# From the tenth attention step on: a stated order for TensorE

## The chip, the cores and the metric

The kernel runs on one core of one Trainium2 chip. The metric is the device time of one execution in microseconds (us), as the median of several runs; lower is better. A profiled execution gives, beside its time, a trace of every instruction on the engines: TensorE (PE), VectorE (DVE), ScalarE (ACT), GpSimd (POOL) and SyncE (SP, which issues the transfers).

## What is computed

Four batches of eight heads of attention with a window and 32 global positions, a normalised gated feed-forward layer and a second feed-forward layer with a rational function between its products:

```python
# attention, per batch and head: 512 local and 32 global positions, 64 wide
s_g   = scale * q_g @ k_all.T                      # global rows see all 544 keys
out_g = softmax(s_g) @ v_all
s_l   = scale * q_l @ [k_g, k_l].T                 # local rows: the 32 global keys and |i-j| <= 32
out_l = softmax(masked s_l) @ [v_g, v_l]
x = concat(out_g, out_l) as (B*544, 8*64)          # 2176 rows of 512
# first feed-forward layer
xn = x / sqrt(mean(x*x) + 1e-6) * rms_g
x  = (silu(xn @ w_gate) * (xn @ w_val)) @ w_out    # d_ff 1536
# second
h = x @ w_in                                       # d_ff 2048
x = (P(h) / (Q(h) + 1e-6)) @ w_out2                # cubic over quadratic
```

## The kernel before

**Stages.** The work is in three stages: attention, the first feed-forward layer (class `FFN1`) and the second one (`ffn2`). The loop over `t` in `tile_attn_ffn_kernel` (L889) runs attention in steps and puts the first 58 units of `FFN1` among them (`IN_ATTN`, L878); the other units of `FFN1` follow from L931 on, when the memory of attention has been given to the next weights; then comes `ffn2`.

**Attention in steps.** There are 32 score sets (`NS`), each for two heads and 256 local rows. A set s goes through four parts: `scores` (PE products into psS, then four masked minima on DVE at L401 and four exponentials on ACT at L406), `trans` (four PE transpositions into psT, copied to `pt` by ACT at L413), `pv` (16 small PE products with the values into psO, divided on DVE at L431 to L434 into `on`) and `out` (two transpositions into psX, copied into `x` by ACT at L444). Before a set can start, `make_q` (psQ, copied on ACT) and, for the first four sets of a batch, `make_k` (psK, copied on DVE) have to run; `make_g` (psKG) does the same for a batch's global part, and `g_scores`, `g_trans`, `g_pv` and `g_out` (psG, psGT, psOg, psGX) compute two groups of global rows per batch. A step t of `step` (L519) makes the operands of set t, then takes set t-1 to part 2, set t to part 1, set t-2 to part 3 and set t-3 to part 4; the last steps, t up to 35, only finish what is open (`TAIL`, L146).

**Shapes on PE.** psT, psX, psQ, psK, psGT and all products of `FFN1` use the whole array (128*128 in the rows). psS uses it as tiles of 64*32, psO and psOg of 128*32, psG of 128*64. An attention product in plain float32 has two MATMUL records in the trace, so a whole psS or psO group is 16 products and 32 records.

**FFN1 in units.** A unit is 12 products: half of an `up` (six into psg and six into psv, L650 to L654; two units make one k of one block of rows) or one `down` (12 into psA, L678 to L680). After the second half of an `up`, `act` (L661 to L669) takes psg and psv through ACT (tanh, L665) and DVE (L666, L667) and splits the result in two parts, `ah` on ACT and `al` on POOL. A block's normalisation (`norm_stages`) sums squares on ACT and POOL (L609 to L615), puts the sum over partitions on PE (psN, L618), takes a power on ACT (L620) and six steps on DVE (L623 to L625), scales the four parts of `x` on DVE (L628); `split` then makes `xt` in two parts on ACT (L640) and POOL (L641). The blocks follow in the order 1, 0, 3, 2, 5, 4, 7, 6, twelve units each (eight in the first).

**Banks.** Eight PSUM banks are shared in three kinds: four "big" (psS, psG, psg, psv), two "t" (psT, psQ, psK, psX, psGT, psGX, psKG) and two "o" (psO, psOg, psA, psN). Who writes a bank waits until the engine that reads its last content is done.

**What sets the order.** The program is recorded in the order of the code, and a scheduler with its own estimate of times then places the instructions on each engine; `tc.high_priority` shifts some of them forward. `between()` (L874) puts a unit in where the target number for this step has not been reached. So, on PE, instructions of attention and of feed-forward units can stand between each other singly.

Of the kernel before, what the change touches and what calls it, by code (L numbers as in the profile page):

```python
# [19 lines left out]
B, H, SL, SG, D = 4, 8, 512, 32, 64  # L20
# [118 lines left out]
class Attention:  # L139
# [3 lines left out]

    NP = B * H // 2
    NS = 2 * NP
    TAIL = 4  # L146
    VW = 65

    def __init__(self, tc, pool, x, stage, q_l, k_l, v_l, q_g, k_g, v_g, more):
# [367 lines left out]
    def step(self, t, between):  # L517
# [30 lines left out]
        for q0, first in ((0, 4), (1, 5)):  # L548
            n = i - first
            if t < NS:  # L550
# [7 lines left out]
                if n == 2:  # L558
# [3 lines left out]
                    between()  # L562
                    self.g_out(qd)


class FFN1:

# [236 lines left out]
def kernel(  # L804
# [20 lines left out]
    def load_consts():  # L825
        nc.sync.dma_start(out=gam, in_=rms_g.rearrange("(c p) -> p c", p=128))
        nc.sync.dma_start(out=av, in_=bass.AP(tensor=ca.tensor, offset=ca.offset, ap=[[0, 128], [1, 4]]))
        nc.sync.dma_start(out=bv, in_=bass.AP(tensor=cb.tensor, offset=cb.offset, ap=[[0, 128], [1, 2]]))
# [24 lines left out]
    ORD = [2 * b + 1 - i for b in range(B) for i in range(2)]  # L853
    done = [0]
    norms = []
    silu = [False]

    def norm_step():
        if norms and next(norms[0], StopIteration) is StopIteration:
            norms.pop(0)  # L860

    def unit():
        done[0] += 1
        next(units, None)
# [5 lines left out]
    att = Attention(tc, apool, x, y[0].rearrange("p c t -> p (c t)"), q_l, k_l, v_l, q_g, k_g, v_g, more)  # L870
    target = [0]

    def between():
        if done[0] < target[0]:  # L874
            unit()

    LAST = att.NS + att.TAIL - 1
    START, SECOND, IN_ATTN = 5, 9, 58  # L878
    nc.scalar.preload_act_table_set("exp_and_others")
    ps_scope = ExitStack()  # L880
    pp = ps_scope.enter_context(tc.tile_pool(name="ps1", bufs=1, space=PSUM))
# [4 lines left out]
    ffn = FFN1(tc, f1pool, x, y, gam, wts)  # L886
    units = ffn.units([(g, blk, lambda: silu[0]) for g in range(3) for blk in ORD])
    ffn.set_psum(pp, ("big", banks[0]), ("o", banks[2]))
    for t in range(LAST + 1):  # L889
        if t >= SECOND:  # L890
            target[0] = 6 + (IN_ATTN - 6) * (t + 1 - SECOND) / (LAST + 1 - SECOND)
        elif t >= START:
            target[0] = 6 * (t + 1 - START) / (SECOND - START)
        gate = [i.ins for i in (att.last_exp, att.last_ttr) if i]
        with tc.high_priority(offset=50) if t >= START else nullcontext():
            att.step(t, between)
        while done[0] < target[0] - 1:
            unit()
        if t == 2:
            load_consts()  # L900
        if t % 4 == 2 and t > 12:
            norms.append(ffn.norm(ORD[(t - 6) // 4]))
        elif t in (4, 8):
            norms.append(ffn.norm(ORD[t // 4 - 1]))
        with tc.high_priority(offset=200):
            for _ in range(3):
                norm_step()
        for _ in range(2 if t else 0):
            if loads:
                loads.pop(0)()  # L910
        with ExitStack() as late:
            for i in gate if t <= 8 else ():
                late.enter_context(tc.issue_after(i))
            for _ in range((0, 0, 0, 2, 5, 4, 4, 4)[t] if t < 8 else 2):
                wts.step(nc.gpsimd)
    while done[0] < IN_ATTN:
        unit()
    ps_scope.close()
    attn_scope.close()

# [88 lines left out]
```

## Time and profile before

| | us |
|---|---|
| median of 3 runs | 1047.36 |
| lowest and highest | 1046.0, 1047.61 |
| the profiled execution, its own time | 1044.23 |
| the span of its instructions | 1042.5 |
| PE busy | 985.7 (95%) |
| DVE, ACT, POOL busy | 784.3, 595.0, 272.7 |

The profiled execution took 1.7 us more than the span of its instructions, and 3.1 us less than the median. In the trace the tenth step (t = 9) begins at about 92 us, the last product of attention (psX of set 31) stands at 287.70, and the first product of the first unit of which both programs have the same things before and after it on PE (the third `up` of block 4, psg_4_2) at 303.15. The stretch from 83.18 (psK of set 8's keys, up to where both programs have the same order) to 303.15 is the one in which the change moves PE's work; it holds 1925 products.

### The profile page before, as it was taken

The numbers are of one execution on the slowest core, as the hardware profiler recorded it, in microseconds if no ns is written. First come the engines' busy times: TensorE is split into PE (matmuls) and PEld (weight loads), VectorE is DVE, ScalarE is ACT, GpSimd is POOL, SyncE is SP. The second block draws the span as 40 slices with busy tenths as digits, with TensorE's granted clock in tenths as the row PEclk, the third lists the DMA queues.
The fourth block names the chain that finished last, engine by engine and source line by source line (L and its number), as shares of the span: only waits on it lengthen the run. The fifth ranks groups of instructions, "written<-read, shape, count | busy, mean of one in ns | idle before, by whom it ended". The sixth has DMA issues, their size and how long they took to land.

```text
span 1042.5 us, 21627 instructions
## 1 busy us (share of the span) xinstructions
PE 985.7 (95%) x8352; PEld 883.7 (85%) x8352; DVE 784.3 (75%) x1842; ACT 595.0 (57%) x1347; POOL 272.7 (26%) x337
## 2 busy tenths in 40 slices
PE   6488999999989999999999999999999999999997
PEld 5266777677789999999999998898989889888895
DVE  5776456546479898855885535898998989989897
ACT  4665556455476764544644323666666667666674
POOL 6344131222200000000000003343443444434433
PEclk9679999999989999999999999999999999999999
DMA  9735545353081413523501116000000000000000
GB/s 243 226 85 130 118 120 119 84 130 81 7 304 45 157 43 131 200 95 107 177 1 42 41 31 225 29 1 20 11 2 31 1 1 31 1 31 1 1 31 21
DMA packets 103303, 82.25 MB, mean 79 GB/s; under 512 B 63136, under 2 KB 90784, under 8 KB 103200
## 3 DMA queue, kind: packets, MB, share of 16 engines
q1 hardware_dynamic: 101472, 74.58, 24.5%
q0 software_dynamic: 1728, 6.29, 1.8%
q8 instruction: 66, 1.08, 0.5%
q14 instruction: 37, 0.30, 0.1%
HBM read 62.64 MB, written 10.75 MB: 70 GB/s over the span
## 4 chain that ended last, share of the span: by engine, by line
PE 60%; DVE 20%; ACT 7%; DMA 5%; POOL 4%; issue 2%; SPq 2%; ACTq 0%; POOLq 0%; DVEq 0%
PE psg L650 4%; PE psA L678 4%; PE psg L654 4%; PE psv L654 4%; PE psv L650 4%; PE psA L680 4%; PE psv L651 4%; PE psA L679 4%; PE psg L651 4%; DVE q L772 3%; DVE q L760 3%; DVE r L773 3%; DVE p L774 3%; PE psH L750 2%; PE psH L751 2%
## 5 line engine op out<-in xcount | busy, mean ns | idle before, releaser
L750 PE MATMUL psH<-yt,w_h 128*128 128x384 f32 (+1 forms) x384 | 126.0, 329 | 1.2 <-ACT yt L732 0.7
L751 PE MATMUL psH<-yt,w_h 128*128 128x384 f32 (+1 forms) x384 | 125.4, 327 | 0.0
L752 PE MATMUL psH<-yt,w_h 128*128 128x384 f32 (+1 forms) x384 | 123.4, 328 | 0.8 <-DVE yt L733 0.8
L678 PE MATMUL psA<-ah,w_o 128*128 128x288 f32 (+1 forms) x384 | 112.2, 295 | 4.9 <-ACT ah L668 1.8
L650 PE MATMUL psg<-xt,w_g 128*128 128x288 f32 (+1 forms) x384 | 113.9, 300 | 0.9 <-ACT xt L640 0.9
L134 POOL TENSOR_SCALAR gh<-p 128x384 fp32r<-128x384 f32 (+1 forms) x96 | 59.4, 618 | 209.5 <-DVE p L774 180.3
L785 PE MATMUL psB<-w_p,gh 128*128 128x512 f32 x272 | 108.2, 398 | 5.4 <-POOL gh L134 5.1
L650 PE MATMUL psv<-xt,w_v 128*128 128x288 f32 (+1 forms) x384 | 111.2, 292 | 0.5 <-ACT a L663 0.5
L651 PE MATMUL psv<-xt,w_v 128*128 128x288 f32 (+1 forms) x384 | 111.1, 291 | 0.0
L651 PE MATMUL psg<-xt,w_g 128*128 128x288 f32 (+1 forms) x384 | 110.8, 291 | 0.0
L776 POOL TENSOR_TENSOR gl<-p,gh 128x384 fp32r<-128x384 f32 (+1 forms) x96 | 108.4, 1129 | 8.4 <-PE psB L787 0.4
L679 PE MATMUL psA<-ah,w_o 128*128 128x288 f32 (+1 forms) x384 | 110.2, 290 | 0.0
L680 PE MATMUL psA<-al,w_o 128*128 128x288 f32 (+1 forms) x384 | 109.8, 290 | 0.0
L786 PE MATMUL psB<-w_p,gh 128*128 128x512 f32 x272 | 107.2, 394 | 0.0
L654 PE MATMUL psv<-xt,w_v 128*128 128x288 f32 (+1 forms) x384 | 105.0, 293 | 0.0
L654 PE MATMUL psg<-xt,w_g 128*128 128x288 f32 (+1 forms) x384 | 104.7, 294 | 0.0
L770 ACT ACTIVATE r<-q,cq 128x384 f32<-128x384 f32 (+1 forms) x96 | 57.4, 598 | 63.5 <-DVE q L760 62.6
L91 POOL TENSOR_SCALAR raw_h<-raw_h 128x512 int32<-128x512 uint32 x1 | 0.6, 647 | 335.0 <-DMA raw_h<-in_moe_w_in_dram 335.0
L760 DVE SCALAR_TENSOR_TENSOR q<-q,bv,t 128x384 f32<-128x384 f32 (+1 forms) x96 | 67.4, 702 | 22.2 <-ACT q L758 21.9
L787 PE MATMUL psB<-w_p,gl 128*128 128x512 f32 x272 | 82.0, 394 | 0.0
L759 ACT ACTIVATE p<-psH,av 128x384 f32<-128x384 f32 (+1 forms) x96 | 62.8, 654 | 29.5 <-POOL gl L776 29.3
L678 PEld LDWEIGHTS psA<-ah,w_o 128*128 128x128 f32 x384 | 72.6, 190 | 7.6 <-ACT ah L668 2.3
(172 smaller groups left out, 2684.7 us busy)
## 6 DMA issues: line engine op xcount, KB each, us to landing
raw_h<-in_moe_w_in_dram SPq DMA_DIRECT2D x16, 512.0 KB, 4.0
raw_p<-in_moe_w_out_dram SPq DMA_DIRECT2D x16, 512.0 KB, 4.6
vw<-vw SPq DMA_DIRECT2D x56, 130.0 KB, 2.5
raw_g<-in_moe_w_gate_dram SPq DMA_DIRECT2D x12, 512.0 KB, 6.2
raw_v<-in_moe_w_val_dram SPq DMA_DIRECT2D x12, 512.0 KB, 6.6
raw_o<-in_moe_w_out_dram SPq DMA_DIRECT2D x12, 512.0 KB, 6.8
vw<-in_v_l_dram SPq DMA_DIRECT2D x62, 80.0 KB, 2.6
out_dram<-o SPq DMA_DIRECT2D x17, 256.0 KB, 2.0
```

The lines of the kernel that those rows point to most:

```text
L650: nc.tensor.matmul(ps[j], part(j, 0, c), xt[c][:, 0], start=(c == 0), stop=False)
L651: nc.tensor.matmul(ps[j], part(j, 1, c), xt[c][:, 0], start=False, stop=False)
L654: nc.tensor.matmul(ps[j], part(j, 0, c), xt[c][:, 1], start=False, stop=(c == 3))
L678: nc.tensor.matmul(ps, wh, ah, start=(i == 0), stop=False)
L679: nc.tensor.matmul(ps, wl, ah, start=False, stop=False)
L680: nc.tensor.matmul(ps, wh, al, start=False, stop=(i == 3))
L750: nc.tensor.matmul(ph[:, :n], wh, yt[:, c, 0, :n], start=(c == 0), stop=False)
L751: nc.tensor.matmul(ph[:, :n], wl, yt[:, c, 0, :n], start=False, stop=False)
L752: nc.tensor.matmul(ph[:, :n], wh, yt[:, c, 1, :n], start=False, stop=(c == 3))
L776: nc.gpsimd.tensor_tensor(out=gl[:, :n], in0=p, in1=gh[:, :n].bitcast(F32), op=ALU.subtract)
L785: nc.tensor.matmul(acc[m], gh[:, sl], wh, start=(k == 0), stop=False)
L786: nc.tensor.matmul(acc[m], gh[:, sl], wl, start=False, stop=False)
```

## The change

`TAIL` becomes 2, so attention has 34 steps in place of 36. From `FLOW` = 9 on, PE's instructions are recorded under `tc.manual_schedule` and keep the order of the code up to the end of the 58 units; the scheduler still places those of the other engines. The steps from there on are made by a new function `flow`, in which set t-1 is taken to part 2, set t to part 1, set t-2 to part 4 and set t-1 to part 3 (before: t-2 to part 3, t-3 to part 4), the operands of set t+1 are made in step t (`ready`), and units stand in three places between whole groups. A block's normalisation is started one step earlier (t % 4 == 1), and from step 9 on it advances by two stages per step, one of them inside `flow`, in place of three.

```diff
-    TAIL = 4
+    TAIL = 2
...
+    def ready(self, t):
+        b, i = divmod(t, 8)
+        if t >= self.NS:
+            return
+        if i == 0:
+            self.make_g(b)
+        self.make_q(t)
+        if i < 4:
+            self.make_k(4 * b + i)
+
+    def flow(self, t, between, middle):
+        NS = self.NS
+        b, i = divmod(t, 8)
+        live = t < NS
+        qd = 2 * b
+        if live and t + 1 < NS:
+            self.spread_v(t + 1)
+        self.advance(t - 1, 2)
+        between()
+        if live and i in (6, 7):
+            self.g_pv(qd + i - 6)
+            if i == 6:
+                self.load_vn(2 * qd + 3)
+        if live and i in (5, 6):
+            self.g_trans(qd + i - 5, 0)
+        self.advance(t, 1)
+        if live and i in (5, 6):
+            self.g_trans(qd + i - 5, 1)
+        self.advance(t - 2, 4)
+        self.advance(t - 1, 3)
+        if live and i == 4 and b + 1 < B:
+            self.load_g(b + 1)
+        if live and i in (3, 4, 5):
+            self.load_vn(4 * b + i - 3)
+        self.ready(t + 1)
+        between()
+        middle()
+        if live and i in (4, 5):
+            self.g_scores(qd + i - 4)
+        if i == 0 and b:
+            self.g_out(qd - 1)
+        if live and i == 7:
+            self.g_out(qd)
+        between()
...
-    START, SECOND, IN_ATTN = 5, 9, 58
+    START, SECOND, IN_ATTN, FLOW = 5, 9, 58, 9
...
+        if t == FLOW:
+            manual.enter_context(tc.manual_schedule(engines={mybir.EngineType.PE}))
+            att.ready(t)
...
-            att.step(t, between)
+            if t >= FLOW:
+                att.flow(t, between, norm_step)
+            else:
+                att.step(t, between)
...
-        if t % 4 == 2 and t > 12:
-            norms.append(ffn.norm(ORD[(t - 6) // 4]))
+        if t % 4 == 1 and t > 12:
+            norms.append(ffn.norm(ORD[(t - 5) // 4]))
...
-            for _ in range(3):
+            for _ in range(3 if t < FLOW else 1):
                 norm_step()
...
+    manual.close()
```

What it does to PE's order is shown at three places, as the built programs have it. In the names the first number after psS, psT, psX, psO, psQ is the set, after psA group, block and part, after psg, psv and xt the block and the k or the group; the last number is a buffer. The lines of `FFN1` are 47 higher in the changed program (L697 is L650 of before, L725 is L678, L665 is L618).

The first place is in the eleventh and twelfth steps, the end of a feed-forward unit, the scores of set 11 and the transpositions of set 10. Before, on PE:

```order
L654 MATMUL psv_0_0_1430<-xt0_0_2_1390,w_v_0_665 128x288
L680 MATMUL psA0_1_1_1689<-al1_2_1177,w_o_2_1133 128x256
L678 MATMUL psA0_1_1_1689<-ah1_3_1397,w_o_3_1303 128x256
L654 MATMUL psg_0_0_1429<-xt0_0_3_1393,w_g_0_658 128x288
L679 MATMUL psA0_1_1_1689<-ah1_3_1397,w_o_3_1303 128x256
L654 MATMUL psv_0_0_1430<-xt0_0_3_1393,w_v_0_665 128x288
L388 MATMUL psS11_0_1552<-kt3_95,qt11_1523 32x128
L411 MATMUL psT10_1531<-ident_112,p10_1461 128x128 x2
L388 MATMUL psS11_1_1553<-kt3_95,qt11_1523 32x128
L411 MATMUL psT10_1531<-ident_112,p10_1461 128x128
L388 MATMUL psS11_0_1552<-kt3_95,qt11_1523 32x128
L411 MATMUL psT10_1531<-ident_112,p10_1461 128x128
```

And now, on PE, the same transpositions between the end of a `down` and the next unit:

```order
L725 MATMUL psA0_1_0_1558<-ah1_3_1438,w_o_3_1303 128x256
L726 MATMUL psA0_1_0_1558<-ah1_3_1438,w_o_3_1303 128x256
L727 MATMUL psA0_1_0_1558<-al1_3_1439,w_o_3_1303 128x256
L411 MATMUL psT10_1574<-ident_112,p10_1506 128x128 x4
L697 MATMUL psg_0_1_1581<-xt0_0_0_1347,w_g_1_678 128x288
L698 MATMUL psg_0_1_1581<-xt0_0_0_1347,w_g_1_678 128x288
L697 MATMUL psv_0_1_1582<-xt0_0_0_1347,w_v_1_798 128x288
```

Before, single scores and transpositions alternate, and the unit ahead is mixed with a `down`; now the four transpositions stand together between two whole units, and the 16 scores of set 11 follow the second one without a break.

The second place is the first unit of block 0, which needs that block's normalisation (psN of block 0). On PE before, from that psN on:

```order
L618 MATMUL psN0_1289<-st0_0_1279,ones_208 128x288
L411 MATMUL psT8_1324<-ident_112,p8_1270 128x128
L331 MATMUL psK6_1404<-ident_112,kin0_87 128x128 x4
L411 MATMUL psT8_1324<-ident_112,p8_1270 128x128 x3
L331 MATMUL psQ10_1413<-ident_112,qin0_89 128x128 x2
L411 MATMUL psT9_1422<-ident_112,p9_1369 128x128 x4
L421 MATMUL psO8_1490<-vw0_100,pt8_1329 32x65
L678 MATMUL psA0_1_0_1538<-ah1_0_769,w_o_0_1113 128x256
L679 MATMUL psA0_1_0_1538<-ah1_0_769,w_o_0_1113 128x256
```

These go on with the rest of that `down`, the keys and the queries of the next sets and psO of sets 8 and 9, and then comes psg_0_0. On PE now, the end of the last unit of block 1 and what follows it:

```order
L701 MATMUL psg_1_3_1333<-xt0_1_2_707,w_g_3_956 128x256
L701 MATMUL psv_1_3_1334<-xt0_1_2_707,w_v_3_963 128x256
L701 MATMUL psg_1_3_1333<-xt0_1_3_710,w_g_3_956 128x256
L701 MATMUL psv_1_3_1334<-xt0_1_3_710,w_v_3_963 128x256
L697 MATMUL psg_0_0_1445<-xt0_0_0_1347,w_g_0_658 128x288
L698 MATMUL psg_0_0_1445<-xt0_0_0_1347,w_g_0_658 128x288
L697 MATMUL psv_0_0_1446<-xt0_0_0_1347,w_v_0_665 128x288
L698 MATMUL psv_0_0_1446<-xt0_0_0_1347,w_v_0_665 128x288
```

The `down` psA0_1_0 that stood between the psN and psg_0_0 comes after psg_0_0 now; what stands between them is half of the scores of set 9, psO of set 8, one psQ, one psK and the 12 products whose end is shown.

The third place is the end of attention. On PE before:

```order
L421 MATMUL psO30_4259<-vw2_102,pt30_4113 32x65 x16
L503 MATMUL psGX7_4220<-ident_112,og7_4218 128x128
L411 MATMUL psT31_4224<-ident_112,p31_4147 128x128 x4
L440 MATMUL psX29_4280<-ident_112,on29_4189 128x128 x2
L421 MATMUL psO31_4324<-vw3_103,pt31_4229 32x65 x16
L440 MATMUL psX30_4345<-ident_112,on30_4278 128x128 x2
L440 MATMUL psX31_4389<-ident_112,on31_4343 128x128 x2
L618 MATMUL psN6_4403<-st0_6_4393,ones_208 128x288
L678 MATMUL psA0_5_0_4478<-ah5_0_3839,w_o_0_1113 128x256
```

On PE now, from the middle of the unit behind psX of set 31:

```order
L698 MATMUL psv_4_0_4378<-xt0_4_3_4362,w_v_0_665 128x288
L701 MATMUL psg_4_0_4377<-xt0_4_2_4359,w_g_0_658 128x288
L701 MATMUL psv_4_0_4378<-xt0_4_2_4359,w_v_0_665 128x288
L701 MATMUL psg_4_0_4377<-xt0_4_3_4362,w_g_0_658 128x288
L701 MATMUL psv_4_0_4378<-xt0_4_3_4362,w_v_0_665 128x288
L665 MATMUL psN6_4467<-st0_6_4415,ones_208 128x288
L725 MATMUL psA0_5_0_4471<-ah5_0_3775,w_o_0_1113 128x256
```

Before, psO of set 31, psX of sets 30 and 31, the psN of block 6 and the next `down` follow each other with nothing between; now the two units of psg_4_0 and psv_4_0 stand around psX31, ahead of psN.

Counted in the built orders between psK of set 8 and psg_4_2, a piece being products of one kind that follow each other: psS stands in 46 pieces before and 25 now, psO in 48 and 25, psOg in 16 and 6, and feed-forward products in 78 and 52.

## Rows read from the trace of the kernel before

**Rows 1.** The page's first line: span and instructions.

```profile
span 1042.5 us, 21627 instructions
```

**Rows 2.** Busy time (instructions) per engine in the stretch, granted PE clock, DMA share.

```profile
83.18:303.15 219.97, 205.37 (x2861) 162.07 (x2861) 122.34 (x482) 117.33 (x320) 55.20 (x73) 0.98 0.47 117
```

**Rows 3.** PE groups in the stretch: name xcount | busy us, mean ns | idle before.

```profile
L388 PE MATMUL psS<-kt,qt 64*32 64x128 f32 x768 | 24.4, 276 | 0.6 <-ACT qt L356 0.5
L421 PE MATMUL psO<-vw,pt 128*32 128x65 f32 x800 | 23.1, 224 | 0.8 <-ACT pt L413 0.5 <-PE psOg L484 0.2
```

**Rows 4.** PE in order of time: start, us, what, xrecords; split and whole groups.

```profile
116.02 0.67 PE L388 MATMUL psS<-kt,qt 64*32 64x128 f32 x32
116.62 0.43 PE L421 MATMUL psO<-vw,pt 128*32 128x65 f32 x16
...
122.28 0.41 PE L421 MATMUL psO<-vw,pt 128*32 128x65 f32 x10
122.63 0.44 PE L440 MATMUL psX<-ident,on 128*128 128x128 f32 x2
123.00 0.66 PE L421 MATMUL psO<-vw,pt 128*32 128x65 f32 x32
123.59 0.63 PE L477 MATMUL psGT<-ident,pg 128*128 128x128 f32 x3
...
131.40 0.42 PE L388 MATMUL psS<-kt,qt 64*32 64x128 f32 x8
131.75 0.40 PE L650 MATMUL psg<-xt,w_g 128*128 128x288 f32 x1
131.99 0.30 PE L651 MATMUL psg<-xt,w_g 128*128 128x288 f32 x1
132.12 0.30 PE L650 MATMUL psv<-xt,w_v 128*128 128x288 f32 x1
...
133.55 0.64 PE L388 MATMUL psS<-kt,qt 64*32 64x128 f32 x24
134.12 0.40 PE L650 MATMUL psg<-xt,w_g 128*128 128x288 f32 x1
```

**Rows 5.** Who on PE waited for whom in the stretch: us, times, longest.

```profile
PE psT L411 <- ACT qt L356: 1.7, 3, 0.7
...
PE psQ L331 <- ACT x L444: 0.9, 2, 0.5
```

**Rows 6.** PE, DVE and ACT in order of time: block 0 from psN to xt.

```profile
93.33 0.75 PE L618 MATMUL psN<-st,ones 128*128 128x288 f32 x2
...
100.25 0.51 DVE L628 SCALAR_TENSOR_TENSOR x<-x,gam,st 128x288 f32<-128x288 f32 x1
...
100.79 1.30 ACT L640 ACTIVATE xt<-x 128x288 fp32r<-128x288 f32 x3
```

**Rows 7.** PE, ACT and DVE in order of time: a unit's end to its banks' release.

```profile
107.08 0.30 PE L654 MATMUL psv<-xt,w_v 128*128 128x288 f32 x1
...
107.17 0.41 ACT L665 ACTIVATE a<-psg 128x288 f32<-128x288 f32 x1 [1.45 <-PE psg L654]
...
108.18 0.45 DVE L667 SCALAR_TENSOR_TENSOR a<-a,psv 128x288 f32<-128x288 f32 x1
```

**Rows 8.** PE at the end of attention; then a window with its granted clock.

```profile
287.70 0.41 PE L440 MATMUL psX<-ident,on 128*128 128x128 f32 x2 [0.68 <-DVE on L434]
290.06 0.97 PE L618 MATMUL psN<-st,ones 128*128 128x288 f32 x2 [1.94 <-POOL st L615]
291.67 0.55 PE L678 MATMUL psA<-ah,w_o 128*128 128x256 f32 x1 [0.64 <-DVE st L619]
...
292.00:294.00 2.00, 2.00 (x11) 2.00 (x11) 1.04 (x3) 1.90 (x4) 0.00 (x0) 0.50 1.03 358
```

**Rows 9.** DVE and PE: the second weight group's last conversion and its first use in a `down`.

```profile
347.38 0.68 DVE L109 TENSOR_TENSOR w_o<-cv,w_o 128x512 fp32r<-128x512 f32 x1
...
365.18 0.28 PE L678 MATMUL psA<-ah,w_o 128*128 128x256 f32 x1
```

More of the change, by code (lines that the diff above doesn't have):

```diff
@@ L888 @@
     ffn.set_psum(pp, ("big", banks[0]), ("o", banks[2]))
+    manual = ExitStack()
     for t in range(LAST + 1):
+        if t == FLOW:
+            manual.enter_context(tc.manual_schedule(engines={mybir.EngineType.PE}))
+            att.ready(t)
         if t >= SECOND:
```

## The prediction, made before the changed kernel ran

> **What bounds the kernel now.** I read the page's overview first, then windows over the stretch in which the two orders differ, then PE's own groups, its timeline and its waits. The whole span is 1042.5 us [rows 1]. In the stretch from 83.18 to 303.15, 219.97 us long, PE is busy for 205.37, DVE for 122.34, ACT for 117.33 and POOL for 55.20, at a granted clock of 0.98 [rows 2]. So PE is the bound there and idle for only 14.6 us; the other engines have 45% or more to spare. What is to be seen next is that busy isn't the same as working: the MATMUL bars overlap, and the distance from one start to the next is the real price. In the stretch stand 768 records of psS and 800 of psO [rows 3], that is 24 and 25 groups of 32 records. A whole psS group takes from 116.02 to 116.62, 0.60 us. One that was cut in two takes 0.35 (131.40 to 131.75, 8 records) and 0.57 (133.55 to 134.12, 24 records), 0.92 in all [rows 4]. The same for psO: 32 records take 0.59, 10 take 0.35 [rows 4]. A straight line through those two is 0.011 us per record and 0.24 per piece; for psS the pieces of 8 and 32 give 0.010 and 0.27. A feed-forward unit pays as well when a piece of attention stands in it: its 12 products from 131.75 to 133.55 take 1.80 us, at an inner distance of 0.13 (131.99 to 132.12) 1.6, so 0.2 for getting in and out [rows 4].
>
> **Term A: fewer pieces.** The counts are those of the built orders. psS goes from 46 pieces to 25: 21 x 0.27 = 5.7. psO from 48 to 25: 23 x 0.24 = 5.5, and I take 0.21, since the shortest pieces of psO give less than the line: 4.8. psOg from 16 to 6, at the same 0.2: 2.0. Feed-forward pieces from 78 to 52: 26 x 0.2 = 5.2, less 0.5 for those that only a transposition divided, which uses the whole array too: 4.7. Sum 17.2 us less on PE. Since PE is 93% busy in the stretch, this is on the path unless new waits take it. Bounds: 12.5 if the 0.2 of the feed-forward pieces is part of the other price and not added to it, 18.5 if the higher prices hold.
>
> **Term B: the end of attention.** Before, psX of set 31 starts at 287.70 after a wait, psN of block 6 at 290.06, and the next `down` at 291.67 [rows 8]: 4 us in which PE does 0.5 us of work. Then the clock is granted at 0.50, the lower level of 1.2 GHz, in the window 292 to 294 [rows 8]. From 291.67 to 303.15 stand 72 products, 48 of 256 columns and 24 of 288; at 0.13 for 288 columns and 8/9 of it for 256 they would take 8.9 us and take 11.5, so the low clock cost 2.6. Now two units of 1.6 us stand around psX31. The chain from psX31 to psN (copy, square, one sum on POOL) took 290.06 - 287.70 = 2.4, so some 0.8 us of waiting is left, and too little idle time for the clock to fall again. Gain: 4.0 - 0.6 (the two matmul groups) - 0.8 + 2.6, about 5.2 us. I take 5. Bounds 2.5 (the clock falls anyhow) and 6.5. The weights of the second group, whose loads start when attention's memory is free, then have less PE work ahead of them by about the 3 us of waits that went: their last conversion ends at 347.38 + 0.68 = 348.1 and is first used at 365.18 [rows 9], 17 us later, and that cover hides the 3 us; without it they would be paid in full.
>
> **Term C: new waits.** PE now stands at whatever its order names next. Four places:
>
> First, block 0's first unit. Before, psN starts at 93.33, the scaled x at 100.25, its first split part on ACT at 100.79 [rows 6]: 7.5 us from psN to the first operand. Now only half a psS (0.3), a psO (0.6), a psQ and a psK (0.7) and one unit (1.6) lie between, 3.2 us. DVE had gaps in that chain and may do it in 6.5, so PE waits 3 to 4.5 us, where before a `down` and two psO filled the time. In place of that filler the filler now comes later, so the wait is a true loss: +3.5.
>
> Second, block 3, whose psN now stands one step (5 to 6 us of PE work) ahead of its first unit, while POOL has four copies of a new batch's keys ahead of the splits. +1.5 over the waits that stand there now.
>
> Third, units that follow each other with little between. A unit's last product starts at 107.08; ACT reads its bank at 107.17 and DVE ends the second product at 108.18 + 0.45 = 108.63 [rows 7]: 1.5 us until the banks are free. At four places the next k of `up` comes after only a transposition group (0.6) or less, since scores hold the other two "big" banks: 4 x 1.0 = +4.
>
> Fourth, the other 20 or so steps. psK needs the bank of a psX that ACT has to copy, 0.6 to 0.8 us of PE work later; psGT waits for two exponentials. Such waits exist before too, 1.7 us for psT and 0.9 for psQ [rows 5], and many go with the old order. +1.
>
> Sum +10. The trace of before can't show a strict order, so the bounds are wide: 0 (what is lost at new places is won at old ones, of which 14.6 us of idle time exist) and +25 (a wait of 1 us in each of 25 steps).
>
> The moved DMAs cost nothing by this: a set's values are loaded when psO of four sets earlier is done, four steps ahead as before, while the spread over partitions now has two steps (14 us) in place of three; the transfers' share is 0.47 [rows 2]. They also move on SP's queue together. On DVE, ACT and POOL nothing is added; two steps fewer at the end hold no work.
>
> **Sum.** -17.2 - 5 + 10 = -12.2 us. The profiled execution, 1044.2 (span 1042.5 and 1.7 around it), becomes 1032.0. The median of the runs shown is 1047.4, 3.1 above it; the same difference gives 1035.2.
>
> **A rule that speaks against it.** psT waits 1.7 us for qt, the copy that empties one of two "t" banks, and psQ 0.9 for x [rows 5]; these come back every few steps. The Trainium skill (Perfetto Trace Analysis, Optimization Strategy) says that a gap that repeats on the engine that should be saturated can mean that there isn't enough PSUM for the next tile. By it no order removes these waits and the fourth place costs more, perhaps +5 instead of +1, which gives 1039; by the rows, which show some dozen waits of this kind in 25 steps, I stay with +1.
>
> **The rivals.**
>
> *The waits don't grow* (C = 0): -22.2, 1025. For it: DVE and ACT have time to spare, and a wait at one place lets the next operands catch up, which my sum of places leaves out. Against it: block 0's 3 us of cover for a chain of 7.
>
> *The clock falls at a block's start.* Before, 4 us with little PE work were followed by the low level of 1.2 GHz [rows 8]; a wait of 3.5 at block 0 is close to that, and block 3 is next. Price: 2.6 each, the same 72 products' loss. With both -7, 1040. The Trainium skill (TensorE: Matmul & The Clock Gate, Why this matters for your kernels) warns of throughput drops in mid-kernel after idle gaps between bursts of matmuls; by that rule this is the likelier end, and the trace of the end of attention agrees.
>
> *The pieces' price was cover.* If the 0.2 to 0.3 us per piece hid chains that now show as waits one for one, A is worth nothing and the time stays within 2 us of 1047. For it: 14.6 us of idle time says that PE was often just in time. Against it: most pieces stand ahead of products that waited for nothing.
>
> *ACT's queue holds PE in each step* (slower). The copy that empties psX's bank stands on ACT behind the four exponentials (1.3 us) or behind the split part of the unit's result; psK and psT wait for it, and everything behind them on PE. If each of 25 steps lost 1.6 us, 40 in place of about 16 now, C would be +9 + 24, and the sum +11: 1058. It decides from about 1.2 us per step on. For it: in the strict order psX, psO, psQ and psK follow closely. Against it: ACT is busy for only 117.33 of 219.97 us [rows 2].
>
> That the order isn't kept is excluded: the built program shows it.
>
> **How the numbers follow.** The forecast has 0.42; the clock's fall 0.15; waits that don't grow 0.2; price that was cover 0.1; ACT's queue 0.13. Within 0.2% of 1047.4 is about what a measurement of this kernel can tell from no change. Faster: 0.42 + 0.15 + 0.2 and 0.02 of the cover case, 0.79; same 0.08; slower 0.13. The range leaves out the slower case and a part of the cover case at its upper end and the last of the lower bounds below (-24, from A at 18.5, B at 6.5 and C near 0): 1023 to 1045.
>
> **What would show it.** Right: psS, psO and psOg stand in about 25, 25 and 6 pieces and the stretch to psg_4_2 is 12 us shorter, with nearly all of the difference ahead of that product; the clock stays at the upper level at the end of attention; PE waits 3 us or more at psg_0_0. Wrong: idle time of PE in the stretch over 35 us; or waits for ACT copies ahead of psK in most steps; or a later stage that gives the gain back by waiting for weights.

## The result, and the profile after

The changed kernel takes 1019.88 us (median of 4 runs, 1019.33 to 1021.57) where the kernel before, on the same chip, takes 1046.68 (4 runs, 1044.98 to 1047.61): a ratio of 0.9748, 95% interval 0.9730 to 0.9767. In a second comparison it was 1021.85 and 1043.31, ratio 0.9794 (0.9768 to 0.9821). The forecast was 1035.2 and its range 1023 to 1045: the direction was right, the forecast had under half of the gain, and the time lies below the range.

The first line of the page of after [rows 1], and the window over the stretch from psK4 (the keys of set 8) to psg_4_2 [rows 2]; columns as there: length, then busy us (instructions) of PE, weight loads, DVE, ACT, POOL, then granted PE clock, DMA share, GB/s.

```profile
span 1018.4 us, 21628 instructions
```

```profile
80.33:279.56 199.23, 183.97 (x2861) 157.80 (x2861) 120.06 (x475) 112.34 (x318) 55.69 (x73) 0.96 0.50 124
```

The stretch is 219.97 - 199.23 = 20.74 us shorter, and PE's idle time in it is 199.23 - 183.97 = 15.26, against 14.60 before: the new waits that I forecast did not raise it. The mean clock fell from 0.98 to 0.96. Of the other 3.4 us of the two spans, 2.85 lie ahead of psK4, where the order on all engines is the same in both, and 0.5 behind psg_4_2.

The groups of psS and psO in the stretch [rows 3] (name xcount | busy us, mean ns), then PE in order of time in the step with psS of set 12 [rows 4]:

```profile
L421 PE MATMUL psO<-vw,pt 128*32 128x65 f32 x800 | 16.5, 222 | 0.0
L388 PE MATMUL psS<-kt,qt 64*32 64x128 f32 x768 | 16.4, 275 | 0.0
```

```profile
113.50 0.67 PE L388 MATMUL psS<-kt,qt 64*32 64x128 f32 x32
114.10 0.44 PE L440 MATMUL psX<-ident,on 128*128 128x128 f32 x2
114.47 0.66 PE L421 MATMUL psO<-vw,pt 128*32 128x65 f32 x32
115.06 0.44 PE L331 MATMUL psQ<-ident,qin 128*128 128x128 f32 x2
```

psS is 24.4 to 16.4 us busy, psO 23.1 to 16.5, with as many records: a whole group takes 0.60 and 0.59 from start to start, as the whole ones did before. The waits of PE in the stretch [rows 5], the longest five:

```profile
PE psg L697 <- ACT xt L687: 3.4, 2, 3.1
PE psA L725 <- DVE on L434: 3.2, 1, 3.2
PE psK L331 <- issue: 2.7, 2, 1.3
PE psX L440 <- DVE on L434: 1.9, 2, 1.0
PE psN L665 <- DVE a L714: 1.5, 1, 1.5
```

There are 17 waits in place of 40, counting every gap of PE over 0.02 us (the view lists those over 0.15, 26 before and 17 now, with psK4's at the edge of the stretch), and a few long ones in place of many short ones. The long ones stand at the starts of blocks: psg_0_0 (3.12 at 96.37), psK8, the keys of set 16, and block 3 (1.33 and 0.70, from 139.54 on), psK12, the keys of set 24, and psA0_3_1 (1.34 and 3.23, from 199.61 on). At each of the three the clock falls. Two-microsecond windows about the first and the second:

```profile
94.00:96.00 2.00, 0.00 (x0) 0.00 (x0) 1.96 (x6) 0.54 (x2) 0.56 (x1) 1.00 0.57 131
96.00:98.00 2.00, 1.63 (x7) 1.45 (x8) 2.00 (x3) 1.01 (x3) 2.00 (x3) 0.68 0.66 154
98.00:100.00 2.00, 2.00 (x11) 1.98 (x11) 0.69 (x1) 0.64 (x2) 2.00 (x3) 0.50 0.78 179
...
142.00:144.00 2.00, 1.59 (x7) 1.11 (x6) 1.23 (x3) 0.42 (x1) 2.00 (x3) 0.50 0.28 57
144.00:146.00 2.00, 2.00 (x11) 2.00 (x11) 0.70 (x3) 0.51 (x2) 0.85 (x2) 0.50 0.59 134
```

PE is empty from 94 to 96, and from 98 to 100 it runs at 0.50, the lower level of 1.2 GHz. The same products of a unit there and behind it:

```profile
98.39 0.44 PE L701 MATMUL psg<-xt,w_g 128*128 128x288 f32 x1
98.63 0.44 PE L701 MATMUL psv<-xt,w_v 128*128 128x288 f32 x1
...
100.70 0.29 PE L697 MATMUL psg<-xt,w_g 128*128 128x288 f32 x1
100.83 0.30 PE L698 MATMUL psg<-xt,w_g 128*128 128x288 f32 x1
```

They start 0.24 us apart at the lower level and 0.13 at the upper one, so nearly half of the time at the lower level is lost. In all, products that start at the lower level take 15.8 us of the stretch, 5.7 before. The end of attention is the opposite case [rows 8]:

```profile
266.62 0.38 PE L440 MATMUL psX<-ident,on 128*128 128x128 f32 x2
...
270.10 0.72 PE L665 MATMUL psN<-st,ones 128*128 128x288 f32 x2 [1.51 <-DVE a L714]
270.45 0.50 PE L725 MATMUL psA<-ah,w_o 128*128 128x256 f32 x1
```

```profile
272.00:274.00 2.00, 2.00 (x18) 2.00 (x17) 1.97 (x5) 2.00 (x6) 0.85 (x1) 1.00 1.06 363
```

One wait of 1.51 is left, and the clock stays at the upper level (1.00; 0.50 in [rows 8]).

### The profile page after: what moved, and what is told of

Read it like the earlier page. It is cut to its first block, busy times and chain, and to the rows that moved or that the text cites. A ratio compares the mean times of both kernels' runs of the same rounds, so it can differ in the third digit from the quotient of the medians.

```text
span 1018.4 us, 21628 instructions
## 1 busy us (share of the span) xinstructions
PE 964.2 (95%) x8352; PEld 880.9 (87%) x8352; DVE 785.3 (77%) x1842; ACT 590.9 (58%) x1347; POOL 269.6 (26%) x337
## 4 chain that ended last, share of the span: by engine, by line
PE 73%; DVE 14%; ACT 5%; DMA 3%; POOL 2%; issue 2%; ACTq 0%; POOLq 0%; DVEq 0%
PE psH L799 5%; PE psH L797 5%; PE psB L832 5%; PE psH L798 5%; PE psB L833 5%; PE psB L834 5%; PE psA L725 4%; PE psA L726 4%; PE psA L727 4%; PE psg L697 4%; PE psg L701 4%; PE psv L697 4%; PE psv L701 4%; PE psg L698 4%; PE psv L698 4%
## 5 line engine op out<-in xcount | busy, mean ns | idle before, releaser
L697 PE MATMUL psg<-xt,w_g 128*128 128x288 f32 (+1 forms) x384 | 116.0, 303 | 6.4 <-ACT xt L687 5.9
L725 PE MATMUL psA<-ah,w_o 128*128 128x288 f32 (+1 forms) x384 | 112.2, 296 | 4.0 <-DVE on L434 3.2
L697 PE MATMUL psv<-xt,w_v 128*128 128x288 f32 (+1 forms) x384 | 111.7, 292 | 0.0
L698 PE MATMUL psg<-xt,w_g 128*128 128x288 f32 (+1 forms) x384 | 111.3, 291 | 0.0
L701 PE MATMUL psg<-xt,w_g 128*128 128x288 f32 (+1 forms) x384 | 105.9, 293 | 0.4 <-POOL xt L688 0.4
L697 PEld LDWEIGHTS psg<-xt,w_g 128*128 128x128 f32 x384 | 73.6, 192 | 8.9 <-ACT xt L687 7.3
```

Source lines behind the costliest of these rows:

```text
L697: nc.tensor.matmul(ps[j], part(j, 0, c), xt[c][:, 0], start=(c == 0), stop=False)
L698: nc.tensor.matmul(ps[j], part(j, 1, c), xt[c][:, 0], start=False, stop=False)
L701: nc.tensor.matmul(ps[j], part(j, 0, c), xt[c][:, 1], start=False, stop=(c == 3))
L725: nc.tensor.matmul(ps, wh, ah, start=(i == 0), stop=False)
```

## The experiments

The theory was that whole groups make the gain, by a price for each piece, and that the order pays for it with waits. The rivals were that the pieces only covered waits, and that the new recording (operands a step ahead, three steps deep) makes the gain and not the order. All kernels are compared in the same stretch; "full-clock work" is PE's busy time less half of the time at the lower level (an estimate from the distances just shown), "waits" the number of gaps over 0.02 us, "changes" the number of places where the next product has another tile shape, counted in the built order. All columns but the first are of one profiled execution. The medians come from four comparisons, in which the kernel before had 1043.3 to 1046.7.

| kernel | median us | stretch | idle | at low clock | full-clock work | changes | waits |
|---|---|---|---|---|---|---|---|
| before | 1046.68 | 219.97 | 14.6 | 5.7 | 202.5 | 218 | 40 |
| before again | 1043.80 | 221.18 | 14.4 | 9.7 | 202.0 | 218 | 39 |
| after | 1019.88 | 199.23 | 15.3 | 15.8 | 176.1 | 121 | 17 |
| after again | 1021.85 | 200.36 | 14.8 | 19.6 | 175.8 | 121 | 17 |
| free order | 1031.30 | 205.04 | 8.9 | 13.0 | 189.6 | 205 | 20 |
| old steps, stated | 1040.61 | 216.61 | 24.7 | 15.6 | 184.1 | 127 | 57 |
| scores cut by psX | 1026.34 | 200.90 | 12.8 | 15.7 | 180.2 | 149 | 14 |
| scores cut by a unit | 1033.66 | 211.67 | 19.9 | 14.8 | 184.4 | 167 | 24 |
| units cut by psO | 1029.22 | 204.15 | 19.3 | 9.4 | 180.1 | 122 | 32 |
| bare end | 1030.24 | 208.84 | 21.6 | 19.6 | 177.4 | 121 | 23 |
| operands in the step | 1034.97 | 214.38 | 28.5 | 15.0 | 178.4 | 124 | 35 |
| norm earlier | 1011.04 | 190.27 | 10.8 | 3.3 | 177.8 | 121 | 22 |
| and one unit | 1008.04 | 190.48 | 11.2 | 3.5 | 177.5 | 121 | 23 |
| and q first | 1008.76 | 187.28 | 9.6 | 0.0 | 177.7 | 121 | 22 |

(The free order has 48 feed-forward products less in the stretch, 6.0 us at 0.125 each.)

**The order free again.**

```diff
-            manual.enter_context(tc.manual_schedule(engines={mybir.EngineType.PE}))
```

> The changed kernel recorded as it is, but with the scheduler placing TensorE's instructions again. In the stretch from psK4 to psg_4_2 the built order then has 46 pieces of psS, 46 of psO and 93 feed-forward pieces (25, 25 and 52 in the stated order, 46, 48 and 78 before the change). If whole groups are what the change gains: 21 x 0.27 + 21 x 0.21 + 41 x 0.2 = 18 us more than the changed kernel's 1019.9, so about 1038, with only the end of attention (5 us) left of the gain over 1046.7. If the gain came from the new recording (depth, operands made a step ahead, norms spread), and the pieces' price was cover for waits: within 3 us of 1019.9.

Measured: 1031.30, neither end. With the 6.0 us put back, full-clock work is 195.6, 19.5 us above the changed kernel for 84 more changes, 0.23 each. Idle time is 8.9:

```profile
80.48:285.52 205.04, 196.12 (x2811) 156.15 (x2812) 112.38 (x459) 106.73 (x304) 55.00 (x73) 0.97 0.44 106
```

So the scheduler's mixing does cover waits, 15.3 - 8.9 = 6.4 us of them, and pays 19.5 us of PE for it. The rival was right that there is cover, and wrong by a factor of three on its worth. The recording alone, with the order free, is worth 13 us against the kernel before in its own comparison (1044.21, ratio 0.9878, 0.9835 to 0.9922). So about half of the gain (ratio 0.9748 and 0.9794 with the stated order) comes without it.

**The old steps with a stated order.** Set t's operands in step t, psO of t-2, psX of t-3, `TAIL` 4 as before, norms spread as after:

```diff
+        if t == FLOW:
+            manual.enter_context(tc.manual_schedule(engines={mybir.EngineType.PE}))
...
+        middle()
         self.advance(t - 2, 3)
         self.advance(t - 3, 4)
```

> The kernel before with its old function step and its old depth (set t-2 to part 3, t-3 to part 4, operands of set t made in step t), but with TensorE's order stated from the tenth step on, and the norms spread as in the changed kernel. Pieces: 25 of psS, 25 of psO, 50 of feed-forward units. If whole groups are nearly all of the gain, about 1020 to 1025. If a stated order also needs the operands a step ahead (my term for new waits, here without the change's cure): psQ and psK stand directly ahead of the scores that read their copies, 0.6 to 0.7 us of copy plus the engine's queue, 24 steps x 1.0 = 24 us more idle time on TensorE, about 1044, with many low-clock periods on top.

Measured: 1040.61, ratio 0.9968 (0.9944 to 0.9991). Pieces are as few as after, and most of the gain isn't there (the kernel before against itself gave an interval of 0.9974 to 1.0038): 57 waits, 24.7 us of idle time, among them

```profile
PE psGX L503 <- DVE og L496: 4.6, 6, 1.5
PE psT L411 <- ACT qt L356: 3.9, 8, 0.5
PE psK L331 <- DVE x L507: 3.6, 3, 2.3
```

This fits a stated order that needs steps in which each product was made ready a step earlier; the next kernel asks for the operands alone. Full-clock work is 8.0 above the changed kernel with only 6 more changes but 40 more waits: a wait costs PE about 0.17 us beyond its idle time. The trace has it singly too: the last transposition ahead of a wait takes 0.27 us from its start to where the idle time begins, one ahead of another transposition takes 0.11 from start to start. (Where idle time begins is the profile's: it models the ends of PE's products.)

**Operands in their own step.** Only `ready` moves:

```diff
+        self.ready(t)
         self.advance(t, 1)
...
-        self.ready(t + 1)
         between()
```

> The changed kernel with psKG, psQ and psK of a set moved from the step before to directly ahead of its scores, nothing else moved. If the waits stayed small because the operands are made a step ahead: each of 23 scores then waits for ScalarE's copy of psQ (0.36) or VectorE's of psK (0.66) with what is queued ahead of them, about 0.7 a step, 16 us more idle time in the stretch, 1036 to 1040. If the engines that copy have so much time to spare that the place doesn't matter: under 5 us more.

Measured: 1034.97, 15 us more; the stretch 15.15, idle time 13.3 more. PE's waits and one of the places:

```profile
PE psS L388 <- DVE kt L344: 7.6, 9, 1.2
PE psS L388 <- ACT qt L356: 6.1, 12, 0.7
PE psg L697 <- ACT xt L687: 4.7, 3, 3.3
...
PE psS L388 <- POOL kt L346: 2.7, 2, 1.3
```

```profile
158.51 0.38 PE L331 MATMUL psQ<-ident,qin 128*128 128x128 f32 x2
158.72 0.60 PE L331 MATMUL psK<-ident,kin 128*128 128x128 f32 x4
160.20 0.67 PE L388 MATMUL psS<-kt,qt 64*32 64x128 f32 x32 [0.88 <-DVE kt L344]
```

7.6 + 6.1 + 2.7 = 16.4 us at 23 scores, 0.7 each as expected. This is why the idle time didn't grow: `ready(t + 1)`. The 5.6 us between this kernel and the old steps belong to the depth of the steps or the earlier start of the norms; neither was tested alone.

**Scores cut in two, by psX and by a unit.**

```diff
         for c in range(2):
+            if c and cut:
+                cut()
             for j in range(4):
```

with `cut` taking set t-2 to part 4 in the first kernel, and `between` in the second.

> The changed kernel with each whole psS group cut in two by the psX group that otherwise follows it (psS, psX, psS, psO in place of psS, psX, psO): 22 more pieces of psS, the same products, nothing else moved. If a piece has a price of its own, as the sum had it: 22 x 0.27 = 5.9 us more, about 1025.8 (at 0.2 a piece 1024.3). If the price of a piece was only cover for waits: 1019.9, within 1 us.

> The changed kernel with each psS group cut in two by the unit that otherwise stands ahead of it (psT, half psS, unit, half psS, psX in place of psT, unit, psS, psX): 23 more pieces of psS, no more pieces of units, but 46 more places where the tile's shape changes (167 in place of 121). By a price per psS piece alone (0.27, term A): 6.2 us more. By a price per change of shape, 0.165 (from the cut by psX) to 0.23 (from the kernel before): 7.6 to 10.7 us more in the stretch, net of waits. By cover: nothing, or a gain where the scores' second half lets VectorE start earlier.

Measured: 1026.34 and 1033.66. A cut step of the first kernel:

```profile
114.76 0.45 PE L390 MATMUL psS<-kt,qt 64*32 64x128 f32 x16
115.14 0.44 PE L442 MATMUL psX<-ident,on 128*128 128x128 f32 x2
115.51 0.45 PE L390 MATMUL psS<-kt,qt 64*32 64x128 f32 x16
115.89 0.66 PE L423 MATMUL psO<-vw,pt 128*32 128x65 f32 x32
```

Two halves of 0.38 in place of 0.60: 0.16 for the cut. Over the stretch, full-clock work is 4.1 more; with three waits fewer (0.5) that is 4.6 for 28 more changes, 0.16 each. Only 1.7 of the 6.5 us of the median are in the stretch (2.4 us less idle time stand against the 4.1); 1.1 lie ahead of it and 3.3 behind it, where a `down` and an `up` of the next group wait for ACT (4.8 us from 380 to 480, against 2.7 in the changed kernel): the size of the median agrees with 5.9 by chance. The second kernel has 8.3 us more, 7.1 without its seven more waits: 0.15 for each of 46 changes, 0.31 for each piece. By itself 7.1 decides nothing: it lies between the 6.2 of a price per piece and the 7.6 to 10.7 of one per change. The two kernels together do: a price per piece would have to be 0.21 in one and 0.31 in the other, a price per change is 0.16 and 0.15. PE pays it whether idle time falls (by 2.4 us in the first) or grows (by 4.6 in the second), so it is a price; in the first a part of it was covered.

**Units cut by psO.**

```diff
+        self.cut()
         for c in cs:
             for j in range(2):
                 nc.tensor.matmul(ps[j], part(j, 0, c), xt[c][:, 1],
...
-        self.advance(t - 1, 3)
+        hold(lambda: self.advance(t - 1, 3))
```

> The changed kernel with each psO group put into the middle of the next unit where that is an `up` (16 places), in place of standing between psX and psQ: 16 more feed-forward pieces, while the number of places where the tile's shape on TensorE changes stays (122 in place of 121). As term A counted, with 0.2 for each feed-forward piece on top of the price of the attention pieces: 3.2 us more in the stretch. If the price belongs to the change of shape alone (by my reading of the kernels so far about 0.2 each, and every border is already in the count): within 0.5 us in the stretch, apart from waits.

Measured: 1029.22. Of the 9.3 us, 4.9 lie in the stretch: 4.0 more full-clock work and 4.0 more idle time, against 6.4 less at the lower clock. 15 more waits take 2.6 of the 4.0, so 1.4 is left for 16 more pieces of units, below 0.1 each where term A had 0.2.

```profile
113.11 0.66 PE L421 MATMUL psO<-vw,pt 128*32 128x65 f32 x32
113.70 0.40 PE L710 MATMUL psg<-xt,w_g 128*128 128x288 f32 x1
```

psO takes 0.59 there as anywhere. The 1.4 lies between the two expected figures (0.5 and 3.2) and hangs on the 0.17 for a wait, so it speaks for the changes of shape, whose number had stayed, but does not leave the pieces at nothing.

**The end of attention without units.**

```diff
-        if done[0] < target[0]:
+        if done[0] < target[0] and not closing[0]:
...
+        closing[0] = t >= att.NS
```

> The changed kernel without feed-forward units between the last groups of attention (steps 32 and 33); the four or so units that stood there come after the loop. By term B (4 us of idle time at psX31 and psN6, and 2.6 of low clock after it): 4 to 6 us more, 1024 to 1026, with TensorE waiting for set 31's exponentials and copies and the granted clock at 0.5 soon after. If the end of attention was worth nothing because the units would have waited elsewhere: within 1 us of 1019.9.

Measured: 1030.24, 10 us more, twice what term B gives. PE at the end, then a window behind the second of these waits and one behind the third:

```profile
261.95 0.41 PE L440 MATMUL psX<-ident,on 128*128 128x128 f32 x2 [2.31 <-DVE on L434]
...
264.52 0.66 PE L440 MATMUL psX<-ident,on 128*128 128x128 f32 x2 [1.31 <-DVE on L434]
...
278.32 1.30 PE L665 MATMUL psN<-st,ones 128*128 128x288 f32 x2 [2.92 <-DVE a L714]
```

```profile
266.00:268.00 2.00, 2.00 (x12) 2.00 (x11) 0.00 (x0) 1.06 (x3) 0.92 (x2) 0.50 0.73 222
...
280.00:282.00 2.00, 2.00 (x12) 2.00 (x11) 2.00 (x6) 1.85 (x4) 0.38 (x1) 0.50 1.03 414
```

From psS of set 31 to psg_4_2, the same 193 products, it is 34.3 in place of 23.2 us: 5.4 more idle time, the rest mostly two falls of the clock. The units there are worth what B said and more.

**The norm earlier.** In the changed kernel DVE holds up attention at the starts of blocks. DVE, then PE, at block 5:

```profile
199.54 2.73 DVE L675 SCALAR_TENSOR_TENSOR x<-x,gam,st 128x256 f32<-128x256 f32 x4
...
202.99 0.41 DVE L434 TENSOR_TENSOR on<-psO,dn 128x256 f32<-128x256 f32 x1
```

```profile
199.61 0.63 PE L331 MATMUL psK<-ident,kin 128*128 128x128 f32 x4 [1.34 <-issue]
203.46 0.58 PE L725 MATMUL psA<-ah,w_o 128*128 128x256 f32 x1 [3.23 <-DVE on L434]
```

The `down` waits for psO22's bank, which DVE empties behind four scalings of the norm. Moved half a step earlier (`early` is the norm's next stage):

```diff
         self.advance(t - 1, 2)
         between()
+        early()
...
-            for _ in range(3 if t < FLOW else 1):
+            for _ in range(3 if t < FLOW else int(t % 4 == 1)):
```

> The changed kernel with each block's psN and power taken half a step earlier (ahead of the scores, in the place after the first unit of the step) and its six steps and four scalings on VectorE half a step earlier too. In the changed kernel POOL's last sum lies 6 to 9 us ahead of psN of blocks 3, 2, 5 and 4, so psN needn't wait. If the waits at the starts of blocks come from VectorE doing that norm while attention's copies stand behind it: psK8 (1.33), psK12 (1.34), psg_3_0 (0.7) and psA0_3_1 (3.23) shrink by about 5 in all, and the two low-clock periods of 6.8 us at 141 and 202 go, 3.4 each: 12 us less at most, 1010 to 1013. If VectorE only holds up another set's copies instead, the idle time moves and the time stays within 2 us of 1019.9. If the low clock costs nothing of its own, only the 5 us.

Measured: 1011.04 (1010.97 to 1011.31), ratio 0.9677 (0.9662 to 0.9691), below the changed kernel.

```profile
81.24:271.51 190.27, 179.43 (x2861) 152.35 (x2861) 119.26 (x475) 112.19 (x317) 55.45 (x73) 0.99 0.52 129
```

The stretch is 8.96 shorter: 4.4 less idle time and 12.5 us less at the lower clock, worth 6.2, against 1.7 more full-clock work. The falls at blocks 3 and 5 are gone and the one at block 0 is there (98.85, 3.4 us long).

**One unit in the tenth step.**

```diff
-            target[0] = 6 + (IN_ATTN - 6) * (t + 1 - SECOND) / (LAST + 1 - SECOND)
+            target[0] = 6 + (IN_ATTN - 6) * (t + 1 - SECOND) / (LAST + 1 - SECOND) if t > SECOND else 7
```

> The same, and one unit in place of two in the tenth step, so that the first unit of block 0 (psg_0_0, which waits 3.12 us in the changed kernel) comes about a step later, with three units in the next step. If block 0's wait was a chain that any work can cover: 3.1 less idle time and no low clock at 96.71 (3.4 us long, worth 1.7): 4 to 5 us below the kernel with the earlier norm alone. If attention's own copies then lack the unit as cover: no gain, idle time of the same size at psT9 to psK7.

Measured: 1008.04, but 1006.79 to 1011.90, and the stretch is no shorter (190.48) in the profiled execution, which was the longest, 1011.90. In it the wait at psg_0_0 went and another came 10 us later, with its fall of the clock (109.4):

```profile
PE psQ L331 <- DMA qin<-in_q_l_dram: 2.6, 1, 2.6
```

```profile
104.35 0.38 SPq L222 DMA_DIRECT2D qin<-in_q_l_dram  x1
...
105.29 0.46 SPq L222 DMA_DIRECT2D qin<-in_q_l_dram  x1
```

SyncE's queue, which I had costed at nothing, is what comes late next in this execution. With the loads of q moved ahead there:

```diff
-            self.load_q(s + 2)
+            with self.tc.high_priority(offset=400):
+                self.load_q(s + 2)
```

> The kernel with the earlier norm and one unit in the tenth step, with one more edit: the loads of q stand ahead on SyncE's queue. In the kernel without it the wait at psg_0_0 (3.12) went, and psQ12 waited 2.64 us for the load of its q, which SyncE issued at 105.3 behind 15 transfers of values and global operands. If that queue is what came late: the 2.64 go, and with them the low clock at 109 (3.4 us long, 1.7), so about 4 us below the 1008.0, 1004. If other loads then come late in its place (keys, values), or PE waits elsewhere in the same steps: within 1.5 us of 1008.0.

Measured: 1008.76 (1006.77 to 1011.02), no difference in the median. In the profiled execution (1007.40) there is no wait for q and no fall of the clock in the stretch, which is 3.2 us shorter.

```profile
80.99:268.27 187.28, 177.68 (x2860) 150.88 (x2861) 118.06 (x474) 111.16 (x315) 54.91 (x73) 1.00 0.53 131
```

But this compares the longest execution of one kernel with a short one of the other. The other three of the kernel without the edit took 1006.79 to 1008.71, at a mean granted clock of 0.985 to 0.988 (0.981 in the profiled one; 0.983 to 0.986 with the edit). So the late q need not stand in a usual execution, and a gain from moving the loads is not shown.

**Both kernels again.**

> The kernel before itself once more, for its profile: TensorE's order is the same in both kernels up to psK4, which started at 83.18 before and at 80.33 after, with 34.1 and 27.3 us of low clock ahead of it. If that 2.85 us is chance of an execution, psK4 lies here somewhere in 80.3 to 83.2. If it belongs to the kernel before, it starts at about 83.2 again.

> The changed kernel itself once more, beside the kernel before on the same chip: 1019.9 within 2 us, the low clock again at the three starts of blocks (about 97, 141 and 202), psK4 between 80.3 and 81.6 as in the kernels that share its order there, and the time behind psg_4_2 between 738 and 742 us, if the spread of that part (737.8 to 742.2 so far) is one of executions; 738.8 again if it belongs to each program.

Measured: psK4 starts at 80.72 in the kernel before this time (83.18 in the first profile) and at 80.52 in the changed one. The 2.85 us ahead of the stretch were chance of an execution: the kernel before has 27.3 us at the lower clock there this time, 34.1 in the first profile. The stretches are 221.18 and 200.36, 20.8 apart, as in the first pair (20.7). Behind psg_4_2 stand 739.4 and 739.3 us (739.3 and 738.8 in the first pair), which leaves the 742 of some of the other kernels, each profiled once, unexplained. The executions of the kernel before range from 1037.8 to 1048.1 in this comparison, so its median moves by more than the changed kernel's.

## Why the prediction was wrong

The firm figure is 20.7 to 20.8 us in the stretch, where the sum had 12.2; another 3 to 6 us of the first comparison are executions' chance ahead of the stretch and in the median of before. Taken from the 1047.4 of the prediction, 20.8 gives 1026.6, inside the range; but the sum was 8.6 us short. By terms, in the first pair, each product's time going from its start to the next one's without idle time:

| | predicted | measured |
|---|---|---|
| psS, psO, psOg, units, at full clock | -17.2 | -18.9 |
| transpositions, at full clock | 0 | -7.4 |
| idle time (C, and what B took off) | +7.6 | +0.7 |
| lower clock | -2.6 | +5.0 |
| sum | -12.2 | -20.6 |

Two steps failed by about as much: the idle time, 6.9 us off, and the transpositions, which had no term, 7.4. The lower clock went 7.6 the other way and hid one of the two; without that luck the sum would have been about 16 us short.

**Term A** held in size, and for a reason that was partly wrong. psS gave 6.5 (5.7 predicted), psO 4.9 (4.8), psOg 2.0 (2.0), the units 5.5 (4.7). But the cuts show a price for each change of shape, 0.15 to 0.16 between whole halves and 0.23 in the mixed orders, and next to none for a unit's piece by itself: I had booked under two names what is one border. By that count, 97 changes less at 0.23 (the price of the free order) are 22.3, and 23 waits less at 0.17 (that of the old steps) are 3.9: 26.2, against the measured 202.5 - 176.1 = 26.4. Why a change costs more in the mixed orders is not shown.

**The missing term**, one of the two steps, is that of the transpositions, 7.4 us. My sum only counted the groups whose pieces I had listed, and took a wait at its idle time. Before, 32 transpositions stood ahead of a wait and took 0.28 each without the idle time; after, there are 11. 21 less at 0.28 - 0.11 are 3.6 us. 46 (15 before) stand ahead of a unit and take 0.03, but the unit's first product then takes 0.21 in place of 0.125: the two take 0.24 together, as much as 0.11 and 0.125 apart. So 31 more of these pairs, at 0.08, only move 2.5 of the 7.4 us here from the units' row; the rest stands at borders with attention's products. The pairs also show that a change of work without a change of shape costs nothing there.

**Term B** was right: idle time at the end went from 3.7 to 2.4 us and the clock stayed up, about 4 us where I took 5; without units in the changed kernel's end 10 are lost. (The 72 products at the upper level come to 8.7 us by the prediction's own figures, not 8.9.)

**Term C is the other step that failed.** Its first place was right (psg_0_0: 3.5 predicted, 3.12 measured), the second too (block 3: 1.5; 2.0 with psK8). The third, 4.0, isn't there: I let the second `up` wait for the first one's banks, but it gets the banks of the scores before it. psg_2_3 follows psg_2_2 with only psT between, waits for the minima of set 25, and those ended at 217.4, 2.4 us ahead of its start; in the whole stretch psg waits for xt alone. The fourth, "+1", had the wrong sign: waits outside the listed places and the end were 10.9 us before and are 3.1 after. Two rows of before that have no like after:

```profile
PE psA L678 <- DVE og L496: 1.4, 1, 1.4
PE psT L411 <- DVE ptg L478: 1.1, 2, 0.6
```

I had written that many of these waits go with the old order, and put nothing for it into the sum; the kernel with the operands in their own step has 13 us more idle time, so making them a step ahead is what keeps it down. I had not listed block 5, 4.6 us by psK12 and psA0_3_1, where four scalings on DVE stand ahead of attention. In all C came to 3.1 + 2.0 + 0 - 7.8 + 4.6 = +1.9 us, where I had +10.

The Trainium skill (Perfetto Trace Analysis, Optimization Strategy), by which repeated gaps may mean that there is not enough PSUM for the next tile, would have put C higher still. The trace disagrees here: with the same eight banks, the repeated waits fell from 10.9 to 3.1 us when the order and the depth changed.

**The rivals.** "Waits don't grow" came nearest (1025). "The clock falls at a block's start" happened too, three times, 15.8 - 5.7 = 10.1 us more at half speed, 5.0 us; moving the norm took two of them away and gave it back. The Trainium skill (TensorE: Matmul & The Clock Gate, Why this matters for your kernels) warns of this after idle gaps; the trace agrees, and at the end of attention a wait of 1.51 us brought no fall. I gave these two rivals one case each, as if only one could come; both did, with opposite signs. "Cover" is worth 6.4 us against 19.5. ACT's queue did not hold PE in each step: psK, psQ and psT wait 2.0 us in all for its copies.

## What to carry to other kernels

Count the places where the tile's shape changes and the number of waits, beside the idle microseconds: each of both has a price on PE that no idle column shows. An order written by hand pays where each operand is made a step ahead; with the old steps it gave almost nothing, and the new recording with the order left free gave half. When it is in place, look for the few long waits that are left, since those also cost the clock, and then ask which queue (here DVE's norm) is late next.

## What the runs showed of the hardware

A wait of PE costs about 0.17 us more than the idle time beside it: 40 more waits and 6 more changes made 8.0 us of full-clock work in the kernel with old steps. A change of tile shape costs 0.15 to 0.16 us between whole halves of scores (46 and 28 changes) and 0.23 in the free order (84 changes). From a transposition to a unit, both of 128*128, there is no such price. A stop of 3.1 us (psg_0_0), and one of 2.64 (psQ12), were each followed by 3.4 us at the lower clock; the waits of 0.25 to 1.33 at 23 scores in the kernel with operands in their own step were not, its lower-clock periods lie at the three starts of blocks (97, 145 and 209 us). At block 3 of the changed kernel the clock fell behind waits of 1.33 and 0.29, at the end of attention it did not behind one of 1.51, so the length of one wait does not decide it.
